# The end of an attention-decode kernel: last products bank by bank, last values load in four pieces

## Chip, cores, metric

One core of one Trainium2 chip. The metric is the device time of one execution in microseconds (us), on the slowest core, which here is the only one. A time is given as the median of several executions. Every profile is of one execution and counts its own microseconds from the start of its span; a span is about 2 us shorter than the device time of the same execution (188.0 against 189.86 us for the kernel before). A transfer is taken as landed at the last of its 16 landing records, counted here as one for each of the core's 16 DMA engines: those of the last wo piece in the kernel before go from 182.86 to 184.70, and the products that wait for it start at 184.74. Single landings and starts are read from the trace's records; their last digit can differ by 0.01 from the rounded rows shown.

## The reference

The input row is normalised once and then goes through two branches, which are added to it: attention with one query over a window of 4096 cached keys and values (2 batches, 8 key/value heads, 16 query heads, head size 256), and a dense layer. Cut to what matters here:

```python
q = (x @ wq).reshape(B, Sq, Hq, Dh).transpose(0, 2, 1, 3)
k = repeat(k_cache[:, :, Sk - W:, :], rep, axis=1)      # W = 4096, rep = 2
v = repeat(v_cache[:, :, Sk - W:, :], rep, axis=1)
p = softmax(einsum("bhqd,bhkd->bhqk", q, k) * Dh ** -0.5)
o = einsum("bhqk,bhkd->bhqd", p, v)
out = x + o.transpose(...).reshape(B, Sq, Hq * Dh) @ wo + dense(x)     # (2, 1, 448)
```

## The kernel before

The kernel loads k, v and the output weights wo of one key/value head after another on a single queue. All results gather in PSUM in `psA`: the 448 output columns are cut into four parts of 112, and each part has its own 32 partitions (a quadrant), so that four small products can run side by side: in the profile the first four of the last products start between 184.509 and 184.519, each about 0.25 us long. Each tile of `psA` is counted here as one PSUM bank: parts 0 and 1 lie in one, parts 2 and 3 in another.

```python
    psA = [ps_a.tile([P, DO], FP32, name=f"psA{u}") for u in range(2)]

    def part(n):
        return psA[n // 2][n * Q : n * Q + Bsz, :]

    def add(lhsT, w, start=False, stop=False):
        for n in range(NO):                      # NO = 4, DO = 112
            nc.tensor.matmul(part(n), lhsT=lhsT, rhs=w[:, n * DO : (n + 1) * DO],
                             start=start, stop=stop, tile_position=(0, n * Q), ...)
```

For the last two heads the values are taken with v as the stationary operand: 64 positions t and two halves c give 128 pairs of weight load and product per head.

```python
    def values_fixed(i):
        ...
        for t in range(T):                       # T = 64
            ...
            for c in range(ND):                  # ND = 2
                nc.tensor.matmul(po[:, c, :], lhsT=vv[:, t, c, :], rhs=pTv[:, th, 0:Q:HS], ...)
        scale_o(i, po)                           # VectorE: oT = po * 1/sum

    def mix(kvh):                                # the head's products with wo
        for h in range(rep):                     # rep = 2
            for c in range(ND):
                add(oT[:, c, h, :], w[:, h, c * D : (c + 1) * D], stop=...)
```

The last head's loads, and the end:

```python
            load_v(i, (0, T) if i < Hkv - 1 else (0, T // 2, 7 * T // 8, T))
            load_wo(i, parts=1 if i < Hkv - 1 else 2)
    ...
    res = consts.tile([Bsz, D], BF16)
    for n in range(NO):
        copy = nc.vector.tensor_copy if n // 2 == 0 else nc.scalar.copy
        copy(out=res[:, n * DO : (n + 1) * DO], in_=part(n))
    nc.sync.dma_start(out=out.flatten_outer_dims(), in_=res[:])
```

The softmax here doesn't subtract the row's maximum and nothing guards it: scores larger than these inputs give would overflow.

## Time and profile before

| | kernel before |
|---|---|
| median of the first three executions | 190.17 us (189.82 to 190.4) |
| bytes read from HBM | 77.67 MB, 413 GB/s over the span |
| TensorE, VectorE, ScalarE busy | 75%, 57%, 23% |
| last products start, output issued, span ends | 184.51, 185.75, 188.0 us |

The DMA row and the queue's share of 97% say that the kernel is a stream of bytes; the tail of the timeline says what comes after the stream.

### The profile page before, as it was taken

What the parts mean: (1) busy time and instruction counts of PE and PEld (TensorE: products, weight loads), DVE (VectorE), ACT (ScalarE), POOL (GpSimd) and SP (SyncE); (2) the same over time, 40 slices, a digit from 0 to 9 for tenths busy, and PEclk for the clock granted to TensorE, in tenths of its full rate; (3) what the DMA queues carried; (4) which work ended last, traced back from release to release, by engine and by line L of the source; (5) the groups of instructions that cost most, each with busy time, mean ns of one, the idle gap of its engine ahead of it and who ended that gap; (6) DMA issues with size and microseconds to landing.
All of it is one profiled execution on the core that took longest, in us unless ns stands there. A gap on an engine that the chain in (4) does not pass through costs nothing.

```text
span 188.0 us, 2587 instructions
## 1 busy us (share of the span) xinstructions
PE 140.3 (75%) x1030; PEld 67.3 (36%) x1030; DVE 106.6 (57%) x141; ACT 42.5 (23%) x142; POOL 16.4 (9%) x74
## 2 busy tenths in 40 slices
PE   0396098905989779966795599956996699988863
PEld 0132033903434334423341334422442334433762
DVE  6604497049931994089704991099506983967201
ACT  3004015200440315012421224021511233134101
POOL 7000600300020001100030003000020000000000
PEclk9999659955999978999999969997899969999855
DMA  6999899999999999999999999999999999999991
GB/s 220 421 476 439 383 426 439 446 443 446 432 439 436 399 404 435 439 439 394 474 441 439 418 404 429 432 446 413 452 446 422 398 425 422 457 439 411 411 385 38
DMA packets 5653, 77.83 MB, mean 414 GB/s; under 512 B 517, under 2 KB 2569, under 8 KB 2954
## 3 DMA queue, kind: packets, MB, share of 16 engines
q1 hardware_dynamic: 5636, 77.66, 97.0%
q8 instruction: 8, 0.13, 0.3%
q10 hardware_dynamic: 6, 0.01, 0.0%
q14 instruction: 3, 0.02, 0.0%
HBM read 77.67 MB, written 0.00 MB: 413 GB/s over the span
## 4 chain that ended last, share of the span: by engine, by line
DMA 67%; DVE 19%; PE 11%; SPq 1%; ACT 1%; issue 0%; ACTq 0%; DVEq 0%
DMA k<-in_A_k_cache_dram 57%; DVE kt L373 14%; DMA v<-in_A_v_cache_dram 10%; PE sc L385 6%; PE o L444 4%; DVE pT L411 3%; PE q L494 1%; ACT p L399 1%; PE psA L217 1%; SPq L114 0%; DVE oT L458 0%; DVE sums L420 0%; SPq L349 0%; DVE osum L479 0%; ACTq L591 0%
## 5 line engine op out<-in xcount | busy, mean ns | idle before, releaser
L373 DVE STREAM_TRANSPOSE kt<-k 128x2048 f32<-128x2048 f32 x32 | 73.1, 2288 | 54.3 <-DMA k<-in_A_k_cache_dram 54.3
L385 PE MATMUL sc<-kt,qdiag 128*128 128x512 bf16 x256 | 68.1, 421 | 19.1 <-DVE kt L373 18.1
L399 ACT ACTIVATE p<-sc,off 128x256 bf16<-128x256 f32 x64 | 33.0, 545 | 72.8 <-PE sc L385 72.1
L385 PEld LDWEIGHTS <-qdiag 128*128 128x128 bf16 x256 | 25.5, 105 | 59.0 <-issue 27.1
L444 PE MATMUL o<-v,pT 128*8 128x512 bf16 x192 | 42.5, 379 | 0.0
L444 PEld LDWEIGHTS <-pT 128*8 128x8 bf16 x192 | 17.2, 92 | 22.4
L266 POOL COPY qdiag<-qt 32x16 bf16<-32x16 bf16 x64 | 13.0, 248 | 120.7 <-PE sc L385 103.8
L411 DVE STREAM_TRANSPOSE pT<-p 128x512 bf16<-128x512 bf16 x32 | 21.5, 673 | 2.5 <-ACT p L399 2.4
L399 ACT ACTIVATION_READ_ACCUMULATOR p<-sc,off 128x1 f32 x64 | 11.8, 184 | 0.0
L452 ACT COPY o_sb<-o 8x512 f32<-8x512 f32 x6 | 3.5, 575 | 36.3 <-PE o L444 36.3
L217 PE MATMUL psA<-wo,oT 128*2 128x112 bf16 x128 | 3.3, 229 | 9.5 <-DVE oT L458 9.5
L246 PE MATMUL q_ps<-v,xq 128*128 128x512 bf16 x28 | 8.8, 491 | 2.0 <-DVE xq L237 2.0
L494 PE MATMUL q<-pT,v 128*128 128x4 bf16 x256 | 7.4, 168 | 2.1 <-DMA v<-in_A_v_cache_dram 1.6
L494 PEld LDWEIGHTS <-v 128*128 128x128 bf16 x256 | 7.4, 101 | 2.3 <-DMA v<-in_A_v_cache_dram 1.7
L217 PE MATMUL psA<-v,act_bf 128*2 128x112 bf16 x56 | 1.5, 296 | 6.5 <-DVE act_bf L331 6.5
L256 DVE CAST q_sb<-q_ps 128x512 bf16<-128x512 f32 x2 | 1.3, 684 | 8.3 <-PE q_ps L246 8.3
L246 PEld LDWEIGHTS <-xq 128*128 128x128 bf16 x28 | 3.3, 121 | 7.2 <-issue 3.5
L217 PEld LDWEIGHTS <-oT 128*2 128x2 bf16 x128 | 1.7, 84 | 10.2 <-DVE oT L458 10.2
L180 PE MATMUL xnT_ps<-ident,xn_bf 2*128 2x2 bf16 x7 | 0.5, 165 | 5.7 <-DVE xn_bf L138 5.7
L458 DVE TENSOR_TENSOR oT<-q,rec 128x8 bf16<-128x8 f32 x2 | 0.3, 166 | 7.0 <-PE q L494 7.0
L475 PEld LDWEIGHTS q<-ident_f,o_sb 8*128 8x128 f32 x24 | 3.3, 207 | 2.6 <-issue 2.6
L475 PE MATMUL q<-ident_f,o_sb 8*128 8x8 f32 x24 | 3.8, 264 | 0.0
(54 smaller groups left out, 43.4 us busy)
## 6 DMA issues: line engine op xcount, KB each, us to landing
k<-in_A_k_cache_dram SPq DMA_DIRECT2D x7, 4096.0 KB, 29.5
v<-in_A_v_cache_dram SPq DMA_DIRECT2D x7, 4096.0 KB, 29.5
k<-in_A_k_cache_dram SPq DMA_DIRECT2D x2, 2048.0 KB, 24.5
v<-in_B_w_dram SPq DMA_DIRECT2D x2, 1568.0 KB, 24.0
wo<-in_A_wo_dram SPq DMA_DIRECT2D x7, 448.0 KB, 30.1
v<-in_A_wq_dram SPq DMA_DIRECT2D x1, 2048.0 KB, 7.5
v<-in_A_v_cache_dram SPq DMA_DIRECT2D x1, 2048.0 KB, 15.1
v<-in_A_wq_dram SPq DMA_DIRECT2D x1, 1536.0 KB, 10.7
```

Of the source, the lines that this page charges most:

```text
L217: nc.tensor.matmul(part(n), lhsT=lhsT, rhs=w[:, n * DO : (n + 1) * DO], start=start, stop=stop, tile_position=(0, n * Q), skip_group_check ...
L246: nc.tensor.matmul(ps[u][:], lhsT=xq[:, s, :, :].rearrange("p j k -> p (j k)"), rhs=wq_sb[:, s, u * N5 : (u + 1) * N5], start=(s == 0), st ...
L256: copy(out=q_sb[:, u * N5 : (u + 1) * N5], in_=ps[u][:])
L266: nc.gpsimd.tensor_copy(out=tv[rows, :, e, j * Q : (j + 1) * Q : HS].rearrange("p n (b h) -> p n b h", b=Bsz), in_=qv[rows, :, h0 : h0 + r ...
L373: nc.vector.transpose(out=kt[:].bitcast(FP32), in_=k[:, half * TH * Dh : (half + 1) * TH * Dh].bitcast(FP32),)
L385: nc.tensor.matmul(psc[:], lhsT=qdiag[i % NW][:, n * NE + e, :], rhs=ktv[:, n, e, :, :], start=(n == 0 and e == 0), stop=(n == NB - 1 and ...
L399: nc.scalar.activation(out=pv[:, b, :, :], in_=sv[:, b, :, :], func=ACT.Exp, scale=scale, bias=off[:, b : b + 1], accum_out=state["rs", i] ...
L411: nc.vector.transpose(out=pT[:], in_=p_t.pop(s)[:])
L444: nc.tensor.matmul(po[:], lhsT=pT_t[i * NH + piece][:, uh * NP * Q : (uh + 1) * NP * Q : HS], rhs=v[:, u * NP : (u + 1) * NP, :].rearrange ...
L452: nc.scalar.copy(out=o_sb[:], in_=po[:])
L475: nc.tensor.transpose(pqv[:, u, c, :], ov[:, u, c, :], ident_f[0:NR, 0:NR])
L494: nc.tensor.matmul(po[:, c, :], lhsT=vv[:, t, c, :], rhs=pTv[:, th, 0:Q:HS], start=(t == 0 and c == 0), stop=(t == T - 1), skip_group_chec ...
```

## The change

The intent: let the copies of one PSUM bank run while the products of the other still go on, and have fewer products left to do when the last piece of v lands. The sum's parts now alternate between the banks (0 and 2 in one, 1 and 3 in the other). The second query head of the last group does all products of one bank first. Each bank is copied by both engines, one part each. The last 2 MB of v come as 1.25, 0.5 and 0.25 MB instead of 1.5 and 0.5 MB.

```diff
     def part(n):
-        return psA[n // 2][n * Q : n * Q + Bsz, :]
+        return psA[n % 2][n * Q : n * Q + Bsz, :]
-    def add(lhsT, w, start=False, stop=False):
-        for n in range(NO):
+    def add(lhsT, w, start=False, stop=False, parts=range(NO)):
+        for n in parts:
 ... (in mix)
+        last = kvh == Hkv - 1
+            for bank in ((0, 2), (1, 3)) if last and h == rep - 1 else (range(NO),):
+                for c in range(ND):
+                    add(oT[:, c, h, :], w[:, h, c * D : (c + 1) * D], stop=..., parts=bank)
 ... (last loads and copies)
-            load_v(i, (0, T) if i < Hkv - 1 else (0, T // 2, 7 * T // 8, T))
+            load_v(i, (0, T) if i < Hkv - 1 else (0, T // 2, 13 * T // 16, 15 * T // 16, T))
-    for n in range(NO):
-        copy = nc.vector.tensor_copy if n // 2 == 0 else nc.scalar.copy
+    for n in (0, 2, 1, 3):
+        copy = nc.vector.tensor_copy if n < 2 else nc.scalar.copy
```

More of the change, by code (lines that the diff above doesn't have):

```diff
@@ L506, in mix @@
         w = wo_t.pop(kvh)
+        last = kvh == Hkv - 1
         for h in range(rep):
-            for c in range(ND):
-                add(
-                    oT[:, c, h, :],
-                    w[:, h, c * D : (c + 1) * D],
-                    stop=(kvh == Hkv - 1 and h == rep - 1 and c == ND - 1),
-                )
+            for bank in ((0, 2), (1, 3)) if last and h == rep - 1 else (range(NO),):
+                for c in range(ND):
+                    add(
+                        oT[:, c, h, :],
+                        w[:, h, c * D : (c + 1) * D],
+                        stop=(last and h == rep - 1 and c == ND - 1),
+                        parts=bank,
+                    )
     NFIX = 2
```

## The prediction

> **What bounds the kernel now.** I read the page first, for the balance of the engines. The row of DMA tenths in the 40 slices and the queue table answer it:
>
> ```profile
> DMA  6999899999999999999999999999999999999991
> ...
> q1 hardware_dynamic: 5636, 77.66, 97.0%
> ```
>
> The one large queue keeps the 16 DMA engines busy for 97.0% of the 188.0 us, while TensorE is at 75% and VectorE at 57%. So the kernel streams its caches and weights, and what can be won by other means lies at the two ends of the stream. The change touches only the far end, so I went to the timeline of the last microseconds (columns: start, length, engine, line, operation, output<-input, count, idle before it and what ended it):
>
> ```profile
> 178.69 1.97 PEld L494 LDWEIGHTS <-v 128*128 128x128 bf16 x64
> ...
> 182.33 1.93 PE L494 MATMUL q<-pT,v 128*128 128x4 bf16 x64 [1.58 <-DMA v<-in_A_v_cache_dram]
> 184.29 0.17 DVE L458 TENSOR_TENSOR oT<-q,rec 128x8 bf16<-128x8 f32 x1 [5.03 <-PE q L494]
> 184.51 0.33 PEld L217 LDWEIGHTS <-oT 128*2 128x2 bf16 x16 [0.34 <-DVE oT L458]
> 184.51 0.59 PE L217 MATMUL psA<-wo,oT 128*2 128x112 bf16 x16 [0.26 <-DVE oT L458]
> 185.12 0.56 DVE L563 CAST res<-psA 2x112 bf16<-2x112 f32 x2 [0.67 <-PE psA L217]
> 185.19 0.52 ACT L563 CAST res<-psA 2x112 bf16<-2x112 f32 x2 [10.50 <-PE psA L217]
> 185.75 0.33 SPq L564 DMA_DIRECT2D out_dram<-res  x1
> ```
>
> Read from the bottom: the output leaves at 185.75 and the span ends at 188.0, 2.25 us that the change leaves alone. Before it stand two copies on each engine, before them the 16 last products, before them the scaling, and before that 64 products of the last values, which began when a piece of v landed. The chain of waits tells the same story:
>
> ```profile
> 164.13 18.15 DMA v<-in_A_v_cache_dram
> ...
> 182.33 1.94 PE q L494 x64
> ...
> 184.51 0.69 PE psA L217 x16
> 185.20 0.23 ACT res L563
> ```
>
> Taken alone this chain says: land v earlier and everything moves up. But the 16 products also read wo, whose two last pieces are queued behind v. The issues of the last 28 us, with size and time to landing:
>
> ```profile
> v<-in_A_v_cache_dram SPq DMA_DIRECT2D x1, 1536.0 KB, 18.1
> v<-in_A_v_cache_dram SPq DMA_DIRECT2D x1, 512.0 KB, 18.8
> wo<-in_A_wo_dram SPq DMA_DIRECT2D x2, 224.0 KB, 18.6
> ```
>
> The two wo pieces are issued at about 165.43 and 166.0 (a timeline row of 1.07 us for both), so with 18.6 us each they land at about 184.0 and 184.7. The records of single landings in the trace give it exactly: the last of 16 engines lands the 1.5 MB piece of v at 182.28, the 0.5 MB piece at 183.62, wo's first half at 184.17 and its second half at **184.70**. The instruction records show the 16 products in two halves: the eight of the first head start at 184.51 to 184.57, the eight of the second at **184.745**, and the first of these carries a wait on the second wo piece. The row "x16, idle 0.26 <- oT" merges both and hides it. So the second half of the last products began 0.04 us after the very last transfer of the stream. That is the true bound of the end: not v, but the end of the whole stream.
>
> [...] the 16 landings of the last wo piece go from 182.86 to 184.70, so the slowest engine decides. [...] the 0.5 MB piece is complete 1.34 us after the one ahead of it, and its 8 packets of 4096 B on one engine at about 160 ns account for 1.28 us. [...] the four column tiles of one product set start within 11 ns, and the next set follows about 48 ns after. [...] After the change VectorE and ScalarE read one bank together[...]; before, each had its own bank, so no row yet shows it.
>
> **The change, part by part.**
>
> Last values in four pieces. Before: 2, 1.5 and 0.5 MB; after: 2, 1.25, 0.5 and 0.25 MB. The bytes are the same. On the slowest engine (estimate) 0.25 MB is 8 packets of 2048 B. Packets of 4096 and 1792 B took about 160 and 74 ns, so one costs about 7 ns plus 37 ns per 1000 B, and a 2048 B one 84 ns: the piece takes 0.67 us. Hence the 1.25 MB piece lands at about 182.28 - 0.65 = 181.63, the 0.5 MB piece at 182.95 and the last at 183.69, which is 0.07 us later than the 183.62 of now, as 8 more packets at 7 ns and one more semaphore write of about 8 ns are in the way. TensorE then has 8 products after the last landing in place of 16. Single products follow each other at 27 ns there: start 183.73, last start 183.92, done 184.09 against 184.26. So the values end **0.17 us earlier**, oT with them, and the first eight products at about 184.34 instead of 184.51. But the second eight wait for wo's second half, which comes those 0.07 us later, 184.77: they start at about 184.81 against 184.745. On the path that sets the end the split is worth **+0.07 us**; all of the 0.17 us turns into waiting inside the last products.
>
> One more issue on SyncE, about 0.6 us, pushes the wo issues to about 166; the queue is then still 18 us deep, so it costs nothing. The order of instructions shows that reused DMA semaphores make the late issues wait for older transfers; the youngest of these, the second half of the last k, landed at 162.9, before the first v issue at 163.54. Nothing new.
>
> Products bank by bank. The count stays 16, each with its weight load. Before, the last two sets of four tiles signal their last products at 185.104, 185.138, 185.172 and 185.206 (semaphore records), 34 ns apart, part 0 to part 3; VectorE starts on part 0 at 185.126 and ScalarE on part 2 at 185.195, 23 ns after their signals. Bank 0 is thus not held up by bank 1 by more than these steps. After, bank 0 is parts 0 and 2: their second sets can't start before their first have gone through, 48 ns, so part 0 is done no earlier than now, and part 2 becomes second instead of third to signal. ScalarE starts **0.034 us earlier**; VectorE starts as before. Bank 1 needs one 48 ns set more, but each engine has about 0.27 us of its first copy to hide that. The first copies take about 0.26 us (half of the rows of two), the second follow directly, so the 0.56 and 0.52 us rows keep their lengths. The output waits for the later engine, now ScalarE at 185.72, VectorE at 185.70: a gain of about **0.02 us**.
>
> Elsewhere, parts 0 to 3 now alternate between two banks, in all 188 of the accumulating products (128 + 56 + 4). Outside the tail they are under the stream. Worth 0.
>
> Sum: +0.07 - 0.02, about **+0.05 us**. From 190.17 this is 190.2.
>
> **Rivals.** (1) *v is the bound after all*: wo lands early enough and the 0.17 us count. The page's chain speaks for it; the wait at 184.745 against it. With the bank order it would make about 190.0. In an execution in which wo lands earlier relative to v, part of it may come true, but wo is queued behind v on every engine[...]. (2) *Each added piece costs a fixed time on the stream*: [...] speaks against it that all pieces queue up and land at the engine's own pace (1.34 us for 0.5 MB). (3) *The copies on one bank at once are slower*, or the order by banks stretches the products by another set: 0.05 to 0.3 us, 190.3 to 190.5. (4) *The copies of bank 0 hide fully behind bank 1's products*: at most the 0.1 us between first and last signal, 190.1.
>
> **Range and chances.** All rivals but the second lie within 0.4 us of 190.2. The three runs before went from 189.82 to 190.4, so noise is as large as any of the effects. I take 189.6 to 190.7. For 2%, 3.8 us would be needed, more than the whole tail after the last landing (188.0 - 184.7 = 3.3 us): 0.99 for the same, the rest split evenly.
>
> **What would show it.** In the changed trace: the values' last product ends about 0.17 us earlier relative to the end of the stream; the second head's eight products start within 0.05 us of wo's last landing, with an idle gap of about 0.4 us between the two heads' products; the tail from wo's last landing to the output's issue is 1.03 us, against 1.05 now; ScalarE's first copy no later than 0.06 us after VectorE's. Wrong would be: second-head products that start well after wo landed, copies longer than 0.30 us each, or a stream end that moves by more than 0.2 us for another reason than scatter.

The forecast's sum: +0.07 - 0.02, about +0.05 us, from 190.17 to 190.2. Rival 2 (a fixed time for each added piece) has no time of its own here. That the two engines' copies from one bank would be clean was not shown before the change, nor that wo can't land before v; in both first profiles it landed after it (184.70 after 183.62, and 184.93 after 183.84). The forecast's semaphore write of about 8 ns is 9 ns in the records.

## The result

The changed kernel took 190.0 us (median of 6, 189.8 to 190.67), the kernel before 190.12 us (median of 6, 189.82 to 190.44). The ratio is 0.9999 with a 95% interval of 0.9978 to 1.0019: the same. A ratio is the mean time of one kernel's runs over that of the other's of the same rounds, so it is not quite the ratio of the medians quoted. The forecast of 190.2 and its range hold.

The page of the changed kernel, whose span is 188.2 us, has the same balance:

```profile
DMA  6999999999999999999999999999999999999990
...
q1 hardware_dynamic: 5780, 77.66, 96.9%
```

The packets rose from 5636 to 5780, by 144. By the packet records that is 128 packets of 2048 bytes, the rows of one more piece, and 16 more packets of 4 bytes at 9 ns, as many as the piece has landing records (146 after 160 us instead of 130). The bytes are unchanged. The timeline of the end (start, length, engine, line, operation, count, idle before and what ended it):

```profile
181.69 0.94 PE L495 MATMUL q<-pT,v 128*128 128x4 bf16 x29 [0.94 <-DMA v<-in_A_v_cache_dram]
183.06 1.20 PE L495 MATMUL q<-pT,v 128*128 128x4 bf16 x35 [0.43 <-issue]
...
184.29 0.17 DVE L459 TENSOR_TENSOR oT<-q,rec 128x8 bf16<-128x8 f32 x1 [5.02 <-PE q L495]
184.51 0.18 PEld L218 LDWEIGHTS <-oT 128*2 128x2 bf16 x9 [0.35 <-DVE oT L459]
184.52 0.81 PE L218 MATMUL psA<-wo,oT 128*2 128x112 bf16 x16 [0.26 <-DVE oT L459]
184.97 0.10 PEld L218 LDWEIGHTS <-oT 128*2 128x2 bf16 x7 [0.28 <-issue]
185.35 0.56 DVE L568 CAST res<-psA 2x112 bf16<-2x112 f32 x2 [0.89 <-PE psA L218]
185.38 0.52 ACT L568 CAST res<-psA 2x112 bf16<-2x112 f32 x2 [10.73 <-PE psA L218]
185.97 0.33 SPq L569 DMA_DIRECT2D out_dram<-res  x1
```

The 16 last products now last 0.81 us instead of 0.59, and their weight loads fall into two rows with a gap: the first query head's products start at 184.52, the second's at 184.97. ScalarE's first copy starts 0.03 us after VectorE's instead of 0.07. The chain of waits now names what the chain of the kernel before left out:

```profile
166.68 18.24 DMA wo<-in_A_wo_dram
184.92 0.04 issue
184.97 0.39 PE psA L218 x8
185.36 0.25 DVE res L568
```

The end hangs on the second wo piece, which landed at 184.93, and v is no longer in the chain. There is also a row that the forecast had no place for: 29 products of the last values, then nothing, then 35 products at 183.06 with a pause put down to "issue" (the engine waited for nothing that the profile shows). Those 29 lie within the 1.25 MB piece, which was complete at 181.65, so no data was missing. Here the pause cost nothing: the last 8 products waited for v's last piece all the same (landed at 183.84, they started at 183.88), and wo came later still. The experiments show that it often does cost.

### The profile page after: what moved, and what is told of

The parts are those of the page before. It is cut to its first block, busy times and chain, and to the rows that moved or that the text cites. A ratio compares the mean times of both kernels' runs of the same rounds, so it can differ in the third digit from the quotient of the medians.

```text
span 188.2 us, 2588 instructions
## 1 busy us (share of the span) xinstructions
PE 144.4 (77%) x1030; PEld 68.5 (36%) x1030; DVE 106.3 (56%) x141; ACT 42.5 (23%) x142; POOL 16.5 (9%) x74
## 3 DMA queue, kind: packets, MB, share of 16 engines
q1 hardware_dynamic: 5780, 77.66, 96.9%
## 4 chain that ended last, share of the span: by engine, by line
DMA 67%; DVE 19%; PE 10%; SPq 2%; ACT 1%; issue 1%; DVEq 0%
DMA k<-in_A_k_cache_dram 57%; DVE kt L374 14%; DMA wo<-in_A_wo_dram 10%; PE sc L386 6%; PE o L445 4%; DVE pT L412 3%; SPq L350 1%; ACT p L400 1%; SPq L114 0%; PE psA L218 0%; DVE sums L421 0%; SPq L367 0%; DVE osum L480 0%; DVE oT L459 0%; DVEq L596 0%
## 5 line engine op out<-in xcount | busy, mean ns | idle before, releaser
L386 PE MATMUL sc<-kt,qdiag 128*128 128x512 bf16 x256 | 72.2, 442 | 16.1 <-DVE kt L374 16.0
L386 PEld LDWEIGHTS <-qdiag 128*128 128x128 bf16 x256 | 26.6, 108 | 58.6 <-issue 32.1
L247 PE MATMUL q_ps<-v,xq 128*128 128x512 bf16 x28 | 8.3, 470 | 3.1 <-DMA v<-in_A_wq_dram 3.1
L257 ACT CAST q_sb<-q_ps 128x512 bf16<-128x512 f32 x2 | 1.1, 588 | 13.2 <-PE q_ps L247 13.2
```

The lines of the kernel that those rows point to most:

```text
L247: nc.tensor.matmul(ps[u][:], lhsT=xq[:, s, :, :].rearrange("p j k -> p (j k)"), rhs=wq_sb[:, s, u * N5 : (u + 1) * N5], start=(s == 0), st ...
L257: copy(out=q_sb[:, u * N5 : (u + 1) * N5], in_=ps[u][:])
L386: nc.tensor.matmul(psc[:], lhsT=qdiag[i % NW][:, n * NE + e, :], rhs=ktv[:, n, e, :, :], start=(n == 0 and e == 0), stop=(n == NB - 1 and ...
```

## The experiments

Two theories at first. S: the last landing of wo sets the end, whatever v does. V: v's last piece sets it. Each kernel ran alternately with the kernel before, six executions, with one profile. The first four shared a chip and eleven runs of the kernel before (median 190.28); so did the next four (190.21), then three (190.39), then one (189.97).

### E1 and E2: one part of the change alone

E1 takes only the load cuts, E2 only the bank order:

```diff
 E1, from the kernel before:
-            load_v(i, (0, T) if i < Hkv - 1 else (0, T // 2, 7 * T // 8, T))
+            load_v(i, (0, T) if i < Hkv - 1 else (0, T // 2, 13 * T // 16, 15 * T // 16, T))
 E2, from the changed kernel: the same line the other way round
```

> Last values in four pieces, products and copies as before. Theory S (the last landing of wo ends the stream and sets the end): the second head's products start within 0.05 us of wo's last landing, with at least 0.3 us of waiting between the two heads' products; from that landing to the output's issue 1.05 us as in the kernel before; time 190.1 to 190.3, same. Rival V (v is the bound): no wait between the heads, time 0.2 us below the kernel before, 189.9. Rival F (a piece costs a fixed 0.5 us or more): 190.6 or more.

> Three pieces as before, products and copies bank by bank. Theory S: from the first signal of the last products to the output's issue 0.645 us as in both kernels (0.646 and 0.645), or at most 0.03 us less; first ScalarE copy 0.03 us after VectorE's, against 0.07 before; signals of bank 1 about 0.05 us after those of bank 0; time 190.1, same. Rival (the overlap of bank 0's copies with bank 1's products is worth its full window): output's issue 0.1 us or more sooner after wo's landing, 0.95 us or less in place of 1.05.

E1: 190.35 us (189.69 to 190.66), ratio 1.000 (0.998 to 1.0019). E2: 190.2 us (189.78 to 190.52), ratio 0.9994 (0.9976 to 1.0012). Both the same. E2's small sizes came out as expected: 0.644 us from the first signal of the last products (185.546) to the output's issue (186.19), ScalarE 0.033 us after VectorE, bank 1's signals 0.050 us after bank 0's. Yet from wo's landing (184.79) to the issue it took 1.40 us.

E1's trace shows why, and misses what both theories expected. The second wo piece landed at 184.67, yet the output left at 186.62, **1.95 us** later and not 1.05. Its chain:

```profile
181.69 0.94 PE q L494 x29
182.62 1.46 issue
184.09 1.09 PE q L494 x35
185.18 0.02 issue
185.20 0.18 DVE oT L458
185.38 0.04 issue
185.43 0.65 PE psA L217 x16
```

Again 29 products, then a pause, now until 184.09. The last two pieces of v had been complete since 182.89 and 183.59, and everything behind the pause came late. Neither theory names this wait.

### E3 and E4: both kernels once more

> The changed kernel once more, for a second trace. Theory S: the wait between the two heads' products is there again (0.3 us or more), the distance from wo's last landing to the output's issue 1.04 us again within 0.02. If the engine that also fetched instructions near 180.7 us lands last again, by 0.1 us or more after the other fifteen, the difference of wo's last landing to the kernel before (0.23 us, 0.07 of it foreseen) is that engine's; if not, it is scatter.

> The kernel before once more, for a second trace. Theory S: second head's products within 0.05 us of wo's last landing, 1.05 us from it to the output's issue. Ratio of times 1.000 within 0.003.

E3, the changed kernel: 190.06 us (189.82 to 190.39), ratio 0.999 (0.9973 to 1.0007). Theory S held: second head's products at 185.195, 0.04 us after wo's landing at 185.15, output 1.05 us after it. One DMA engine again landed last, by 0.34 us (fifteen had landed wo by 184.81). Whether it is the one that had carried instructions is not shown; the records don't name engines. E4, the kernel before: 190.39 us (189.68 to 190.84), ratio 0.9999 (0.9979 to 1.002). Here theory S failed, in the very kernel whose first profile had suggested it. wo landed at 184.73, the output left at 186.83, 2.10 us later. The timeline of E4 has the same place:

```profile
182.37 0.94 PE L494 MATMUL q<-pT,v 128*128 128x4 bf16 x29 [0.92 <-DMA v<-in_A_v_cache_dram]
184.30 1.08 PE L494 MATMUL q<-pT,v 128*128 128x4 bf16 x35 [0.99 <-issue]
```

So I formed **theory I**: TensorE runs out of instructions. Counting weight loads from the start of the program, the pause lies after pair 980 in E1, E2, E4 and the changed kernel, and an earlier one, near 177 us, lies after pair 852 in all four. The distance is 128 pairs, which is 256 instructions. The queue of kind "instruction" moves packets of 16,384 bytes; the page of the kernel before counts 8 of them:

```profile
q8 instruction: 8, 0.13, 0.3%
```

So theory I takes one such packet to bring the block of 256 instructions behind one of these points. That is inference: the records show when a packet moved, not what it held. In each of these traces one such packet ended 1.31 to 1.38 us before the pause after pair 980 did (E1: 182.78, then 184.09; E4: 182.94, then 184.30; changed kernel: 181.68, then 183.06).

The packet starts while TensorE still has the 128 pairs between the two points to work off, but by theory I too late. In the first profile of the kernel before, pair 852 passed at 177.14. The next block's packet started at 180.69, ended at 181.63, and from the other traces' 1.35 us its instructions should have been usable at about 183.0 (an estimate). That is 5.9 us for 128 pairs, which TensorE works off in 128 x 27 ns = 3.4 us. Pair 980 was reached at 183.13, so that execution just missed the pause. Whether a pause comes, and how long, goes with when the packet starts: between 2.99 us (E3, no pause) and 4.15 us (E4) after pair 852. Why it starts so late was not shown; the records don't tell when it was asked for.

The packet's time is not the whole of it. Seven traces pause after the old pair 980: the four named, E8 below (0.26 us from start to start, its packet over by 182.17) and the two controls E10 and E12. In five of them TensorE resumes 5.92 us after it started the first pair behind the previous pause (weight loads, start to start), the same within 1 ns, although the packets started 3.45 to 3.64 us after it. In E1 and E4, with packets at 3.96 and 4.15 us, it resumes 0.27 and 0.55 us later than that. So the ends of these seven pauses lie at 5.92, 6.20 and 6.47 us, about 0.27 us apart; what sets them is open.

### E5 to E7: making v the bound

Two other orders test what v's path has to spare. E5 leaves the last 2 MB of v in one piece. E6 and E7 put wo ahead of them, with the cuts of the changed kernel and of the kernel before.

```diff
 E5, from the changed kernel:
-... (0, T // 2, 13 * T // 16, 15 * T // 16, T))
+... (0, T // 2, T))
 E6 and E7:
-                load_v(i, cuts); load_wo(i, parts=2)
+                load_v(i, (0, T // 2))
+                load_wo(i, parts=2)
+                load_cache(v tile, A_v_cache, i, (T // 2, 13 * T // 16, 15 * T // 16, T))   # E7: (T // 2, 7 * T // 8, T)
```

> The changed kernel with the last values in two pieces of 2 MB. Now 64 products of 27 ns stand behind the last landing of v. Theory S with v as a path beside it: v's path is longer by (64 - 8) x 0.027 = 1.5 us, less the 0.45 us it had to spare, so it overtakes wo: no wait for wo between the heads, output's issue about 1.1 us later than in the changed kernel, time 191.0 to 191.4. Rival F (pieces cost a fixed time, so fewer are better): no later than 190.5.

> The changed kernel with both last wo pieces ahead of the second half of the last values, so that v lands last. Theory S: the end then is the last landing of v plus 0.045 + 8 x 0.027 + 0.168 us of products, scaling, both heads' products and copies: about 1.77 us to the output's issue against 1.04, so 0.7 us later than the changed kernel, 190.7 to 191.0; no wait between the heads. Rival V (v is the bound already, wo free): as the changed kernel or better, 190.0.

> As the run before it, but with the three pieces of the kernel before, so that 16 products and not 8 stand behind the last landing. Theory S: here the split is on the path: 8 x 0.027 = 0.21 us more from v's last landing to the output's issue (1.98 us), less 0.07 us of packets, so 0.14 us later than the run with four pieces. Rival (the split is worth nothing in any order): the same distance from landing to issue, 1.77 us.

E5: 190.93 us (190.82 to 191.19), ratio 1.0037 (1.0018 to 1.0057), a little under the forecast. E6: 190.94 us, ratio 1.0034 (1.0016 to 1.0052). E7: 190.98 us, ratio 1.0039 (1.002 to 1.0057). All three are slower by less than the 2% that would count as another class, but clear of 1. From v's last landing at 185.11 to the output's issue at 186.98 it takes 1.87 us in E6 (forecast 1.77), against 1.04 us from wo's last landing in the changed kernel. wo is rightly last in the queue, because less work hangs on it. As a test of theory V, E6 is weaker than its forecast says: putting wo first also moved v's last landing from 183.84 to 185.11, so V too would expect a later end. What speaks against V is the distance. Had v's last landing set the end in the changed kernel, the output would follow it in E6 by the same 2.13 us (183.84 to 185.97). It followed 0.26 us sooner. And in the changed kernel, E3 and E9 the second head's products begin 0.04 us after wo's landing, 0.38 to 0.39 us after the first head's last one started.

Between E6 and E7 the split should show. From landing to issue it took 2.14 us in E7 (184.71 to 186.85), 0.27 us more than in E6 (forecast 0.21). But E7 didn't wait for its last piece: its 64 products ran without a gap from 183.54, behind the landing of the 1.5 MB piece at 183.49, and the 49th, the first that needs the last piece, started at 184.84 when that piece had been there for 0.12 us. So the two traces don't measure the split cleanly. In time the two agree within 0.04 us of median; in the profiled executions E6's stream simply ended 0.40 us later. A saving can't be seen in the total.

### E8: fewer copies behind the stream

```diff
 from the kernel before:
-    psA = [ps_a.tile([P, DO], FP32, name=f"psA{u}") for u in range(2)]
+    psA = ps_a.tile([P, DO], FP32, name="psA")           # all four parts in one bank, zeroed first
-    for n in range(NO): copy = ...; copy(out=res[:, ...], in_=part(n))
-    nc.sync.dma_start(out=out.flatten_outer_dims(), in_=res[:])
+    nc.vector.tensor_copy(out=res[:], in_=psA[:])         # 128 x 112
+    for b, eng in enumerate((nc.sync, nc.scalar)):        # 4 rows of 224 bytes each
+        eng.dma_start(out=out row b, in_=res[b::32])
```

> The kernel before (three pieces, products in their first order) with all four parts of the sum in the four quadrants of one bank, one VectorE copy of 128 x 112 in place of two copies on each of two engines, and the output stored from its four quadrants by two stores, one on SyncE and one on ScalarE. Theory S: only what stands behind the end of the stream shortens the end. One copy of about 0.27 us after the last signal, in place of 0.55: from wo's last landing to the output's issue 0.83 us against 1.05, time about 0.2 us below the kernel before, 189.9, if the two stores take no longer than one. Rival: the stores of four rows of 224 bytes take longer, or the second store's end costs what the copies gave.

190.66 us (190.1 to 190.77), ratio 1.0016 (0.9997 to 1.0036): no gain, and the rival was right. In the profile of E8:

```profile
185.69 0.27 DVE L562 CAST res<-psA 128x112 bf16<-128x112 f32 x1 [0.65 <-PE psA L218]
185.99 0.65 SPq L567 DMA_DIRECT2D out_dram<-res  x1
185.99 0.61 ACTq L567 DMA_DIRECT2D out_dram<-res  x1
```

From wo's landing (185.08) to the issue it took 0.91 us instead of 1.05. The forecast 0.83 was missed because wo didn't set the end in this execution: the short pause after pair 980 held the values up, and the second head's products started 0.15 us after wo's landing and not 0.04. But issuing took 0.61 to 0.65 us instead of 0.33, and from the issue to the end of the span it took 3.0 us (185.99 to 188.98) instead of 2.2. The stores gave back far more than the copies saved.

### E9 to E12: moving the points where instructions run out

If theory I is right, 64 more pairs anywhere ahead move these points by half a block; 128 more put them back on the same old pairs. The extra products are 2 x 2, their result is unused, and they stand in TensorE's idle time after the query projection.

```diff
 E9 and E10 from the changed kernel (64 and 128), E11 and E12 from the kernel before (64 and 128):
     turn(0)
+    pad = ps_q.tile([P, 32], FP32, tag="q", name="pad")
+    for _ in range(64):
+        nc.tensor.matmul(pad[0:Bsz, 0:Bsz], lhsT=ident[0:Bsz, 0:Bsz],
+                         rhs=ident[0:Bsz, 0:Bsz], start=True, stop=True)
```

> The changed kernel with 64 tiny products (2 x 2, result unused) put into TensorE's idle time near 18 us. Theory I: TensorE runs out of instructions where a 16 KB instruction fetch has not come, every 128 pairs of weight load and product (the pauses of six traces lie after pairs 852 and 980); 64 pairs more put these points at 788, 916 and 1044 of the old count, past the end for the last. No pause after pair 980 of the old count in the last head; one at 916 at most, over by about 182; the second head's products wait for wo in every execution, output's issue 1.04 us after wo's last landing; the runs lose their upper end: 189.7 to 190.2 in place of 189.8 to 190.8. Rival (the pauses have another cause, such as TensorE's clock or the DMA): pauses stay after the same products (the old 980).

> As the run before it, with 128 tiny products. Control: theory I says the points fall on the same old pairs (724, 852, 980) as without any, so the pauses after the old 852 and 980 are back in some executions, time as the changed kernel, 189.8 to 190.8. Rival (added early products help in another way): as with 64.

> The kernel before with the 64 tiny products. Theory I: no pause after the old pair 980; values end as soon as v's last piece allows, so the second head's products start within 0.05 us of wo's last landing; output's issue 1.05 us after it; runs 189.7 to 190.2, median about 0.3 us below the kernel before's 190.2. With the same supply of instructions the changed kernel with 64 and this one differ by less than 0.1 us, as wo sets the end in both.

> The kernel before with 128 tiny products, the matched control of the run with 64. Theory I: the points where instructions run out are back on the old pairs (852 and 980), so there are pauses after the new 980 and 1108, and the gain of 64 (ratio 0.9976) is gone: ratio 0.999 to 1.001, runs up to 190.5 or more. Rival (early products help by themselves, whatever their number): ratio 0.998 or lower and no run above 190.1.

| kernel | median (range of 6) | ratio to the kernel before, 95% interval | pause at old pair 980 |
|---|---|---|---|
| E9: changed + 64 | 189.92 (189.80 to 190.06) | 0.998 (0.9967 to 0.9993) | none |
| E10: changed + 128 | 190.06 (189.83 to 190.21) | 0.9986 (0.9974 to 0.9999) | 182.75 to 183.65 |
| E11: before + 64 | 189.83 (189.71 to 190.04) | 0.9976 (0.9964 to 0.9989) | none |
| E12: before + 128 | 190.49 (190.0 to 191.21) | 1.0003 (0.9958 to 1.0047) | 183.57 to 184.68 |

The pauses went where theory I said. The timeline of E11, TensorE alone:

```profile
178.64 0.94 PE L494 MATMUL q<-pT,v 128*128 128x4 bf16 x29 [0.28 <-DMA v<-in_A_v_cache_dram]
180.10 1.07 PE L494 MATMUL q<-pT,v 128*128 128x4 bf16 x35 [0.53 <-issue]
182.37 1.87 PE L494 MATMUL q<-pT,v 128*128 128x4 bf16 x64 [1.20 <-DMA v<-in_A_v_cache_dram]
```

The pause sits 64 pairs earlier, in the first half of the values, where TensorE would have waited for v anyway. The 64 products after it run through in one row. And of E12:

```profile
182.80 0.94 PE L494 MATMUL q<-pT,v 128*128 128x4 bf16 x29 [0.60 <-DMA v<-in_A_v_cache_dram]
184.67 1.07 PE L494 MATMUL q<-pT,v 128*128 128x4 bf16 x35 [0.94 <-issue]
```

With 128 the pause is back after the same 29 products. So where the pause lies goes with the number of added products, and not with their mere presence. In E9 and E11 theory S holds again: second head's products at 184.754 and 184.680, each 0.04 us after wo's landing (184.71 and 184.64), output 1.05 and 1.06 us after it. E11 is the fastest kernel, 0.24% below the kernel before and clear of it, and its runs stay within 0.33 us; since the changed kernel equals the kernel before, it beats that one too, though the two did not run side by side. The comparison of E9 with E10 is weaker in time: E10's interval lies below 1 as well and its runs reach only 190.21, short of the 190.8 that was expected. In the session of E12 one run of the kernel before took 192.58 us (at a granted TensorE clock of 0.733, the lowest of that session), which widens that interval: it contains E11's 0.9976 too. So that the pause moves is shown; that moving it is what makes E11 faster fits its trace, but the times of the two controls don't prove it.

With that pause out of the way, E9 and E11, run in turn on one chip, differ by 0.09 us of median, the changed kernel being the later one. No gain of the change is seen in that setting either.

## Why the prediction was right, and what it missed

**Time and class: right.** 190.0 us against a forecast of 190.2; ratio 0.9999.

**Split of v hidden behind wo: right in the profiled pair.** The gap in the changed kernel between the two heads' products was forecast at about 0.4 us and was 0.39 us, from the start of the first head's last product (184.574) to that of the second head's first (184.966). From wo's landing to the output's issue it was 1.04 us, forecast 1.03. Relative to the stream's end the values were to end 0.17 us earlier by the forecast's list of signs (by its own sum 0.24, since wo comes 0.07 us later), and it was 0.23 us. In absolute time they ended no earlier: 184.09 for the last start in both traces, because v's last piece landed 0.15 us later than forecast; wo landed at 184.93 against 184.70.

**Cost of the extra packets: the +0.07 us drowned in scatter.** The landings of v came at 181.65, 183.22 and 183.84 (forecast 181.63, 182.95, 183.69), those of wo's second half at 184.93 (184.77). A 2048-byte packet took 84 ns, as estimated. The 0.5 MB piece was late on one DMA engine. Fifteen engines had landed it by 182.88, the sixteenth at 183.22, and the same pattern stays to the end (184.65 and 184.93). An instruction packet of 0.93 us ended at 181.68, and the two 4096-byte packets after it took 441 and 373 ns instead of 159. That this is the late engine fits the landing times, fifteen of which advance by about 1.25 us from piece to piece and one by 2.79; the records don't name engines. In the kernel before, an instruction packet of the same length with the same two slow packets behind it left no engine behind at the end (the last two landed wo at 184.66 and 184.70), so there the packet alone made no straggler, and the 0.23 us can't be put down to the change. Over all traces with wo last and three or four pieces, wo's second half landed between 184.64 and 185.17 with three pieces and between 184.67 and 185.15 with four.

**Bank order: +0.02 us forecast, 0.00 measured.** Each of its steps came true: the second sets again started 48 ns after the first (184.966 and 185.014), ScalarE's first copy moved from 0.091 to 0.057 us after the first signal, and VectorE became the last to finish. But from the first signal to the output's issue it is 0.646 us before and 0.645 after, because the issue came 0.03 us after the signal of ScalarE's last copy before and 0.05 us after that of VectorE's now, which ate up the 0.02 us. That wake-up difference I didn't pursue.

**Rivals.** That v is the bound after all is refuted where wo sets the end (the changed kernel, E3, E9) by the second head's wait for wo; that a piece has a large fixed cost by the landing times: the last 0.25 MB was complete 0.70 us after the piece ahead of it in E1 (182.89 and 183.59) and 0.62 us in the changed kernel (183.22 and 183.84). The copies of two engines on one bank in different quadrants ran clean, with correct results and at the old lengths (0.56 and 0.52 us).

**What was missed.** "That is the true bound of the end: not v, but the end of the whole stream" held in the execution at hand, not in general. In E4, the same kernel, the end hung on the pause after pair 980 and came 1.05 us later relative to wo. Of the seven traces with wo last, three or four pieces and no added products, wo set the end in three (both kernels' first profiles and E3), and a pause delayed it in four (E1, E2, E4, E8). That both first profiles were among the three was luck. The class doesn't hang on it, as the pauses meet both kernels. The forecast also took the spread of the runs as noise. Part of it may have a cause: with the pauses moved, twelve runs lie between 189.71 and 190.06, while the kernel before, in turn with them on the same chip, goes from 189.91 to 190.68. But the control E10 on that chip is nearly as narrow (189.83 to 190.21), so this isn't proven. A hint stood in the first profile: a pause of 0.52 us put down to "issue" at 177.13, which I had passed over because it cost nothing there.

## What to carry to other kernels

Before splitting a load to bring a last piece forward, look up in the records what lands last in the whole stream and which instruction waits for it; a row that merges sixteen products hides that wait. Where an engine pauses on "issue" in a run of very short instructions, count instructions from pause to pause. Here it was always the same number (256, of which a pair took 27 ns), and added instructions moved the pause to a place where it cost nothing; having fewer of them was not tried. A second profile of the unchanged kernel costs one run and shows whether the first one's critical path is the usual one.
